# Reversing mirrored filter bins on TensorE: one 192-column matmul in place of three of 64 columns

## Chip, cores, metric

One core of a Trainium2 chip (trn2). The metric is device time in microseconds of one execution. Where I call a kernel faster or slower, the 95% interval of its ratio leaves out 1.

## The reference

The reference alternates two layers twice, each with a residual and a layer norm. Layer A is a global filter in the frequency domain, layer B a two-matmul MLP with Mish.

```python
def _A_ref(x, w_r, w_i):                     # x: 1 x 2048 x 1024
    X = rfft2(x.astype(float32), axes=(-2, -1))
    W = w_r + 1j * w_i                       # 2048 x 513, shared by both A layers
    return irfft2(X * W, s=(2048, 1024)).astype(bfloat16)
# x = x + A(layernorm(x)); x = x + B(layernorm(x)); the same once more
```

## The kernel before

The transforms are matmuls with tables. Work in the frequency domain goes in eight groups `g`, and each group needs its piece of the filter W in a certain order of bins. Of the eight bin classes of a part and a row set, VectorE copies five as they lie. The other three are mirrored: rows and bins come in reverse. The rows (partitions) are reversed by a matmul with an anti-diagonal table `jt`; it writes PSUM, and ScalarE copies that into the second half of each of the first three 128-wide runs of the filter tile `both`. This is done in the first A layer only; the second reloads the finished filter from a scratch tensor in HBM.

The filter tile `wr` is laid out per partition as `[c][s][512]`: real and imaginary part, two row sets, and 512 bins. The 512 bins are 64 blocks `i` of 8 bins `k`, so a bin's position is `8*i + k`. One block is 8 x 2 = 16 bytes. Within the kernel's SBUF buffer the tile starts at a multiple of 16 bytes.

```python
def filter_bins(self, g, ps, banks, wr, wts, off, jt, r_jt, eng):
    both = self.ARENA[:, off // 2:off // 2 + 2048]
    fns = []
    for i in range(2):                                   # row set
        src, j0 = (i, (2, 0)[i]) if g == 0 else (1 - i, 0)
        for c in range(2):                               # real, imaginary
            for kd in (1, 2, 3):                         # one bin class at a time
                col = 512 * i + 192 * c + 64 * (kd - 1)
                mov = wr.ap[:, c, src, :].rearrange("p (i k) -> p k i", k=8)[:, 7 - kd, :]
                fns.append(lambda e, col=col, j=(j0 + c) * P, mov=mov: e.matmul(
                    ps[:, col:col + 64], jt[:, j:j + P], mov, start=True, stop=True))
    self.group(fns, reads=[wr.res, r_jt], writes=banks)
    # ... VectorE copies the bins that are not mirrored (L855) ...
    for i in range(2):                                   # L859 in the profile
        src = ps[:, 512 * i:512 * i + 384].rearrange("p (c k i) -> p c k i", c=2, i=64)
        d3 = both[:, i, :, 0:384].rearrange("p c (k i) -> p c k i", i=P)
        self.op(self.act, lambda e, d3=d3, src=src: e.activation(d3[:, :, :, 64:128], src, ACT.Copy), ...)

# order of a step of the first A layer (cut)
for step in range(11):
    for h in range(2):
        s2(g2, h)                                        # L650: matmuls, then a copy out of PSUM
        if h == 0 and li == 0: filter_bins(g2)           # L844: the matmuls of this study
        s3(g3, h)                                        # L688 to L691
        i1(g4, h)                                        # L717
        i2(g5, h)                                        # L738, L756
```

`self.group` lets only the first matmul wait and only the last one signal. So in each group 12 matmuls of 64 columns run with nothing between them.

Of the kernel before, what the change touches and what calls it, by code (L numbers as in the profile page):

```python
# [5 lines left out]
ACT = mybir.ActivationFunctionType  # L6
ALU = mybir.AluOpType
P = 128
# [171 lines left out]
class KB:  # L180
# [439 lines left out]
    def layer_A(self, li):  # L620
# [177 lines left out]
        for step in range(8 + 3):  # L798
            g2, g3, g4, g5 = step, step - 1, step - 2, step - 3
            for h in range(2):  # L800
                if 0 <= g2 < 8:
                    s2(g2, h)
                if 0 <= g2 < 8 and h == 0 and li == 0:
                    filter_bins(g2)
                if 0 <= g3 < 8:
                    s3(g3, h)
                if 0 <= g4 < 8:
                    i1(g4, h)
                if 0 <= g5 < 8:
                    i2(g5, h)  # L810
                    u_turn(g5, h)
            if 0 <= g3 < 8 and g3 + 2 < 8:
                load_tabs(g3 + 2)
            if li == 0 and g2 + 2 < 8:
                load_w(g2 + 2)
            if li == 0 and 1 <= g2 < 9:
                self.keep_filter(g2 - 1)
            if li and 1 <= g2 < 5:
                load_w(g2 + 3)
            if 0 <= g4 < 8 and g4 + 2 < 8:  # L820
                load_btabs(g4 + 2)
# [12 lines left out]
# [4 lines that stand above are left out]
        for i in range(2):  # L838
            src, j0 = (i, (2, 0)[i]) if g == 0 else (1 - i, 0)
            for c in range(2):  # L840
                for kd in (1, 2, 3):
                    col = 512 * i + 192 * c + 64 * (kd - 1)
                    mov = wr.ap[:, c, src, :].rearrange("p (i k) -> p k i", k=8)[:, 7 - kd, :]
                    fns.append(lambda e, col=col, j=(j0 + c) * P, mov=mov: e.matmul(  # L844
                        ps[:, col:col + 64], jt[:, j:j + P], mov, start=True, stop=True))
        self.group(fns, reads=[wr.res, r_jt], writes=banks)
        for w in wts:
            w.res.begin()
        parts = [w.res for w in wts]
        both = both.rearrange("p (s c k) -> p s c k", s=2, c=2)  # L850
        own = wr.ap.rearrange("p c s (i k) -> p s c k i", k=8)
        for k, n, col in ((0, 4, 0), (7, 1, 448)):
            dst = both[:, :, :, col:512].rearrange("p s c (k i) -> p s c k i", k=n)[:, :, :, :, 0:64]
            src = own[:, :, :, k:k + n, :]
            self.op(eng, lambda e, dst=dst, src=src: e.tensor_copy(dst, src), reads=[wr.res], parts=parts)  # L855
        for i in range(2):
            src = ps[:, 512 * i:512 * i + 384].rearrange("p (c k i) -> p c k i", c=2, i=64)
            d3 = both[:, i, :, 0:384].rearrange("p c (k i) -> p c k i", i=P)
            self.op(self.act, lambda e, d3=d3, src=src: e.activation(d3[:, :, :, 64:128], src, ACT.Copy),  # L859
                    reads=banks, parts=parts)  # L860

    def keep_filter(self, g):
# [234 lines left out]
```

## Time and profile before

| | |
|---|---|
| time, median of 3 runs | 1071.35 us (1070.46 to 1071.45) |
| span of the profiled run | 1068.5 us |
| TensorE busy over the span | 91% |
| first A layer, 50 to 112 us: TensorE, ScalarE, VectorE busy | 100%, 89%, 75% |
| filter matmuls (L844) | 8 groups of 12 x 64 columns |
| stream time of the 8 groups, start to start | 11.0 us |

How to read it: the duration of a matmul in these traces includes a modelled end and overlaps the next one. What a group costs is the time from its first start to the first start of the next line, where TensorE never waits. I call this stream time. The lines are shown in the prediction.

### The profile page before, as it was taken

The page shows a single profiled execution, that of the slowest core. Times are in us where ns is not written, and L with a number is a line of the kernel's source. Part 1 is how long each engine was busy: PE and PEld are TensorE (multiplying, and loading weights), DVE is VectorE, ACT ScalarE, POOL GpSimd, SP SyncE. Part 2 cuts the span into 40 slices and gives each one's busy share as a digit, 9 for nine tenths or more (in the row PEclk, how much of TensorE's full clock was granted, in tenths as well). Part 3 has the DMA queues.
Part 4 walks back from the last instruction along what each step waited for, and adds up shares of the span by engine and source line. Part 5 has one row for each costly group of instructions (what it writes and reads, how often), then busy time and mean ns, then how long its engine had stood idle before and what let it go on. Part 6 is the DMA issues. An engine that isn't in the chain of part 4 may idle for free. (4 is left out here: it accounts for less than half of the span.)

```text
span 1068.5 us, 14145 instructions
## 1 busy us (share of the span) xinstructions
PE 973.0 (91%) x6089; PEld 509.6 (48%) x6089; DVE 362.4 (34%) x811; ACT 330.2 (31%) x466; POOL 55.3 (5%) x86
## 2 busy tenths in 40 slices
PE   0799479999999999999969965999999999999998
PEld 0677345444444444444427744444444444444443
DVE  7887482600444200033436866451011110000111
ACT  6898253342000234300007843434300013431000
POOL 2042000000000000001310200000000000000000
PEclk9699769999999999999988985999999999999999
DMA  9678732444000122211720885144500002210000
GB/s 293 148 247 252 186 111 85 153 150 126 20 20 21 57 68 73 79 60 38 142 47 30 229 200 139 55 143 146 169 22 20 21 34 70 74 40 11 20 20 29
DMA packets 138958, 102.80 MB, mean 96 GB/s; under 512 B 59952, under 2 KB 117552, under 8 KB 138896
## 3 DMA queue, kind: packets, MB, share of 16 engines
q1 hardware_dynamic: 128528, 78.34, 25.1%
q0 software_dynamic: 7856, 22.94, 7.6%
q10 hardware_dynamic: 2512, 0.62, 0.3%
q8 instruction: 48, 0.79, 0.3%
q14 instruction: 14, 0.11, 0.0%
HBM read 80.85 MB, written 20.71 MB: 95 GB/s over the span
## 5 line engine op out<-in xcount | busy, mean ns | idle before, releaser
L930 PE MATMUL PS<-ARENA 128*128 128x512 bf16 x1792 | 393.7, 382 | 1.6 <-DVE ARENA L917 1.6
L948 PE MATMUL PS<-ARENA 128*128 128x512 bf16 x1792 | 390.0, 379 | 0.0
L934 ACT ACTIVATE ARENA<-PS,B 128x512 bf16<-128x512 f32 x224 | 153.8, 687 | 440.0 <-PE PS L930 440.0
L930 PEld LDWEIGHTS PS<-ARENA 128*128 128x128 bf16 x1792 | 175.5, 98 | 214.3 <-issue 6.0
L948 PEld LDWEIGHTS PS<-ARENA 128*128 128x128 bf16 x1792 | 174.5, 98 | 207.8
L953 DVE TENSOR_TENSOR XS<-PS,XS 128x512 bf16<-128x512 f32 x64 | 44.3, 691 | 566.1 <-PE PS L948 566.1
L436 DVE BATCH_NORM_STATS2 BN<-XS 128x6 f32<-128x512 bf16 x108 | 69.5, 673 | 7.5 <-DMA XS<-in_A_x_dram 6.3
L875 PE MATMUL PS<-MT,ARENA 128*128 128x32 bf16 (+1 forms) x768 | 24.7, 189 | 36.1 <-DMA ARENA<-u_scratch 27.9
L881 DVE TENSOR_TENSOR XS<-PS,XS 128x512 bf16<-128x512 f32 (+1 forms) x40 | 29.1, 789 | 75.8 <-PE PS L875 75.8
L575 ACT ACTIVATE ARENA<-PS 128x1024 bf16<-128x1024 f32 x16 | 16.1, 1018 | 110.8 <-PE PS L569 110.6
L875 PEld LDWEIGHTS PS<-MT,ARENA 128*128 128x128 bf16 x768 | 23.0, 101 | 39.5 <-issue 31.4
L417 ACT ACTIVATE ARENA<-XS 128x1024 bf16<-128x1024 bf16 x20 | 21.1, 1056 | 54.6 <-DVE XS L881 43.6
L695 ACT ACTIVATE ARENA<-PS 128x1024 bf16<-128x1024 f32 x32 | 33.0, 1032 | 9.0 <-PE PS L691 9.0
L650 PE MATMUL PS<-FD,ARENA 128*128 128x256 bf16 (+1 forms) x312 | 33.5, 257 | 2.4 <-DVE ARENA L577 2.4
L724 ACT ACTIVATE ARENA<-PS 128x1024 bf16<-128x1024 f32 x32 | 33.0, 1032 | 3.7 <-PE PS L717 3.7
L717 PE MATMUL PS<-ARENA 128*128 128x256 bf16 x256 | 33.2, 273 | 0.1
L699 DVE TENSOR_TENSOR ARENA<-ARENA 128x1024 bf16<-128x1024 bf16 x32 | 22.1, 690 | 28.1 <-ACT ARENA L695 22.7
L650 PEld LDWEIGHTS PS<-FD,ARENA 128*128 128x128 bf16 x312 | 26.3, 99 | 7.2 <-DVE ARENA L577 2.8
L717 PEld LDWEIGHTS PS<-ARENA 128*128 128x128 bf16 x256 | 24.6, 98 | 9.7 <-DVE ARENA L706 0.9
L912 PE MATMUL PS<-IDENT,ARENA 128*128 128x128 bf16 x256 | 21.6, 242 | 8.3 <-DVE ARENA L479 5.8
L738 PE MATMUL PS<-ARENA,BD 128*128 128x256 bf16 x192 | 25.9, 273 | 0.4 <-DVE ARENA L764 0.2
L912 PEld LDWEIGHTS PS<-IDENT,ARENA 128*128 128x128 bf16 x256 | 18.6, 109 | 14.0 <-DVE ARENA L479 6.9
(66 smaller groups left out, 517.8 us busy)
## 6 DMA issues: line engine op xcount, KB each, us to landing
ARENA<-in_B_w_dram SPq DMA_DIRECT2D x56, 512.0 KB, 4.0
ARENA<-in_B_w_dram SPq DMA_DIRECT2D x56, 256.0 KB, 4.4
u_scratch<-ARENA SPq DMA_DIRECT2D x14, 512.0 KB, 4.1
ARENA<-u_scratch SPq DMA_DIRECT2D x14, 512.0 KB, 5.3
XS<-in_A_x_dram SPq DMA_DIRECT2D x4, 1024.0 KB, 8.6
ARENA<-in_A_x_dram SPq DMA_DIRECT2D x32, 128.0 KB, 3.3
w_scratch<-ARENA POOLq DMA_DIRECT2D x8, 512.0 KB, 5.0
ARENA<-w_scratch POOLq DMA_DIRECT2D x8, 512.0 KB, 3.6
```

Source lines behind the costliest of these rows:

```text
L436: self.op(self.dve, lambda e: e.bn_stats(self.BN[:, j, 6 * h:6 * h + 6], self.XS[:, j, 512 * h:512 * h + 512]), reads=[self.r_xs[j]], part ...
L650: fns.append(lambda e: e.matmul(dst, at(r), FD[:, t:t + dst.shape[-1] * 2], start=start, stop=stop))
L695: self.op(act, lambda e: e.activation(x.ap.rearrange("p a b -> p (a b)"), ps, ACT.Copy, scale=SIG), reads=banks, writes=[x.res])
L717: fns.append(lambda e, c=c, part=part: e.matmul(ps[:, c * 256:(c + 1) * 256], yk.ap[:, part, c * P:(c + 1) * P], t[:, (128, 0)[part]:(384, ...
L724: self.op(act, lambda e: e.activation(v.ap[:, :, i, :], src, ACT.Copy), reads=banks, parts=[v.res])
L875: fns.append(lambda e, l=l: e.matmul(ps[:, w * l:w * l + w], self.UT.ap[:, u0 + l, :], self.MT[:, 8 * lo:8 * lo + w], start=True, stop=True))
L881: self.op(self.dve, lambda e: e.tensor_tensor(xs, src, xs, ALU.add), reads=rb, parts=self.r_xs[lo:lo + nb])
L912: fns.append(lambda e, db=db: e.transpose(PSb[:, bank, db * P:(db + 1) * P], xn.ap[:, db * P:(db + 1) * P], self.IDENT[:]))
L930: fns.append(lambda e, db=db, bank=bank, fl=fl: e.matmul(PS[:, bank, :], wb.ap[:, db, fl * P:(fl + 1) * P], x.ap[:, db, :], start=(db == 0 ...
L934: self.op(act, lambda e, bank=bank, ft=ft: e.activation(at.ap[:, ft, :], PS[:, bank, :], ACT.Mish, bias=self.B1[:, ft:ft + 1]), reads=[sel ...
L948: fns.append(lambda e, i=i, ft=ft: e.matmul(PS[:, bank, :], at.ap[:, ft, t * P:(t + 1) * P], W2[ft].ap[:, h * 512:(h + 1) * 512], start=(i ...
L953: self.op(dve, lambda e: e.tensor_tensor(xs, PS[:, bank, :], xs, ALU.add), reads=[self.r_bank[bank]], writes=[self.r_xs[j]])
```

## The change

The intent is to issue fewer and wider matmuls: 32 in place of 96, and as many fewer weight loads. The three bin classes of a part and a row set share the same table, so they can be one matmul with a moving operand of 3 x 64 columns. They are adjacent bins (4, 5, 6), read in ascending order, so the copy out of PSUM writes the classes backwards.

```diff
-                for kd in (1, 2, 3):
-                    col = 512 * i + 192 * c + 64 * (kd - 1)
-                    mov = wr.ap[:, c, src, :].rearrange("p (i k) -> p k i", k=8)[:, 7 - kd, :]
-                    fns.append(lambda e, col=col, j=(j0 + c) * P, mov=mov: e.matmul(
-                        ps[:, col:col + 64], jt[:, j:j + P], mov, start=True, stop=True))
+
+                col = 512 * i + 192 * c
+                mov = wr.ap[:, c, src, :].rearrange("p (i k) -> p k i", k=8)[:, 4:7, :]
+                fns.append(lambda e, col=col, j=(j0 + c) * P, mov=mov: e.matmul(
+                    ps[:, col:col + 192].rearrange("p (k i) -> p k i", i=64), jt[:, j:j + P], mov, start=True, stop=True))
@@
-            self.op(self.act, lambda e, d3=d3, src=src: e.activation(d3[:, :, :, 64:128], src, ACT.Copy),
+            self.op(self.act, lambda e, d3=d3, src=src: e.activation(d3[:, :, ::-1, 64:128], src, ACT.Copy),
```

## The prediction

> **What bounds the kernel now.** I read four views of the profile, in this order. First the page: which engine is full, and when. The busy totals and the slices (each digit is a tenth of the busy share of 26.7 us) give the frame:
>
> ```profile
> PE 973.0 (91%) x6089; PEld 509.6 (48%) x6089; DVE 362.4 (34%) x811; ACT 330.2 (31%) x466; POOL 55.3 (5%) x86
> ...
> PE   0799479999999999999969965999999999999998
> ...
> PEclk9699769999999999999988985999999999999999
> ```
>
> TensorE is the engine to watch, but a share of the whole says nothing of one stage. The changed matmuls run only in the first spectral layer, in slices 2 to 4.
>
> Second, the groups by line, shapes kept apart. The columns are line, engine, operation, operands, shape and count, then busy us and mean ns of one:
>
> ```profile
> L844 PE MATMUL PS<-ARENA 128*128 128x64 bf16 x96 | 12.4, 294 | 0.0
> L875 PE MATMUL PS<-MT,ARENA 128*128 128x64 bf16 x256 | 10.2, 193 | 2.6 <-DVE XS L881 2.6
> L717 PE MATMUL PS<-ARENA 128*128 128x256 bf16 x256 | 33.2, 273 | 0.1
> ```
>
> The first row is the code that changes: 96 matmuls, 8 groups of 12. The second has the same shape, 128x64 with 128x128 weights, yet one takes 193 ns against 294. Even the 256-column matmul of the third is shorter (273). Something other than the count makes L844 dear.
>
> Third, the timeline of TensorE around a group of L844, with the start, the duration and the number of instructions. The modelled durations overlap, so I use starts only:
>
> ```profile
> 71.24 1.05 PE L650 MATMUL PS<-FD,ARENA 128*128 128x256 bf16 x8
> 72.12 1.55 PE L844 MATMUL PS<-ARENA 128*128 128x64 bf16 x12
> 73.50 0.40 PE L688 MATMUL PS<-ARENA 128*128 128x512 bf16 x1
> ...
> 49.17 1.58 PE L844 MATMUL PS<-ARENA 128*128 128x64 bf16 x12
> 50.57 0.39 PE L650 MATMUL PS<-FD,ARENA 128*128 128x256 bf16 x1
> ```
>
> A group takes the stream from 72.12 to 73.50, 1.38 us or 115 ns for each matmul. The very first (49.17 to 50.57) takes 1.40 us, 117 ns each.
>
> Fourth, the table of windows: the length, then busy time and count of PE, PEld, DVE, ACT and POOL, the granted clock and the DMA share:
>
> ```profile
> 50.00:112.00 62.00, 62.00 (x584) 49.38 (x583) 46.25 (x80) 54.98 (x67) 19.77 (x33) 0.99 0.76 234
> ...
> 52.26:53.64 1.38, 1.38 (x15) 1.37 (x13) 0.00 (x0) 1.27 (x2) 1.08 (x2) 1.00 0.49 125
> ...
> 89.31:90.68 1.37, 1.37 (x14) 1.37 (x12) 1.37 (x3) 1.22 (x2) 0.00 (x0) 1.00 1.02 397
> ...
> 49.17:50.57 1.40, 1.40 (x13) 1.40 (x12) 0.83 (x2) 1.02 (x1) 0.21 (x1) 0.50 0.00 0
> ```
>
> From 50 to 112 us TensorE is busy 62.00 of 62.00 us, and the waits of that engine in this window are none. So here a nanosecond of TensorE's stream is a nanosecond of the kernel, unless ScalarE (54.98, 89%) takes over. The groups take the same time with VectorE idle or full and DMA at 0.49 or 1.02, so contention does not make them slow. And the group at a granted clock of 0.50 takes the same as those at 1.00.
>
> **What the Trainium skill says.** (1) "TensorE: Matmul & The Clock Gate", section "Back-to-back issue gap", has N/2.4 + 2.5 ns as the gap of warm matmuls: 29 ns for 64 columns, 109 for 256. The trace agrees for operands that are read in sequence: eight L875 matmuls of 64 columns take 0.25 us in the chain of waits (683.02 to 683.27), 31 ns each; L650's group above takes 0.88 us for 8, 110 ns each. L844 at 115 ns does not fit. (2) The same page, section "LDWEIGHTS", gives 128/1.2 = 107 ns for a weight load, close to what L844's own loads show (117 ns), so one could take L844 for bound by its loads. But L875's loads also last about 100 ns in the trace and are pipelined at 31 ns, so a load does not cost 115 ns of the stream. (3) "SBUF — State Buffer", section "Door 1: The DMA port swizzle", note on cachelines: SBUF has 16-byte lines, successive accesses to one line run at full bandwidth, and "each access that crosses to a new line pays a penalty". The moving operand of L844 takes every eighth bf16, a step of 16 bytes: each column is a new line. No page gives the size of the penalty for a matmul; the trace gives it as (115 - 31)/64 = 1.31 ns per column, if it goes by columns.
>
> That it is a matter of reading and not of the array is what the half-clock group says: before it, at the same clock, the 256-column L650 group that starts at 47.49 takes 1.68 us for 8, 210 ns each instead of 110, while L844 keeps 117 against 115.
>
> **The change part by part.** *Removed:* in each of 8 groups, 12 matmuls and 12 loads become 4 and 4, 64 of each in all. *Added:* each matmul now has 192 columns. The diff writes the operand as (k, i), and i, with the step of 16 bytes, is still the inner one. So the stream still goes to a new line at each column: 64 lines at one k, then 64 at the next. Columns in all: 12 x 64 = 768 before, 4 x 192 = 768 after. *Moved:* the order of the three k turns round, which the ScalarE copy undoes by writing its 64-wide runs backwards. It has the same 384 elements in runs of the same length, so I expect its 488 ns to stay. The order of instructions on the other four engines is the same.
>
> Cost of a 192-column matmul: in sequence it would be 31 + (110 - 31) x 128/192 = 84 ns. With the penalty per column it is 84 + 192 x 1.31 = 335 ns, and four make 1.34 us. Against 12 x 115 = 1.38 us a group saves 0.04 us, and eight save 0.3 us. If all of the 115 ns goes by columns (1.79 ns each), 192 take 344 ns and the saving is nil. If the 31 ns are a part that each matmul pays anew beside its columns, one costs 31 + 192 x 1.31 = 282 ns, four 1.13 us, and eight groups save 8 x 0.25 = 2.0 us. I choose the first: **0.3 us saved**, all on the path because TensorE is full there. The 64 loads that go, 64 x 117 ns = 7.5 us of PEld, lie under matmuls and save nothing.
>
> **The rivals.** *A: the dear part is fixed for each matmul* (a start of a strided read, or the weight load after all). Then a 192-column matmul costs 84 + 84 = 168 ns, a group 0.67 us, and 8 x (1.38 - 0.67) = 5.7 us go; if nothing but the in-sequence pace is left, 8 x (1.38 - 4 x 0.084) = 8.4 us. For it: 115 is near the 117 of a load, and both stay put with the clock. Against it: L875 with as many loads at 31 ns. Time: 1063 to 1066 us. *B: ScalarE takes the saving.* If A holds, ScalarE's 89% allows some 7 us of TensorE's 62 to go before it is the bound, so A would mostly reach the end; for my own 0.3 us it does not matter. *C: the new form is slower*: a copy with a negative step, or a jump back of the operand between planes. The copy may grow without hurting (its consumer is a scratch store and a multiply one step later), and three jumps per matmul replace three instruction starts. At worst 0.1 us per group, about 1 us. *The ceiling:* the eight groups, read start to start, take 1.40 + 4 x 1.37 + 3 x 1.38 = 11.0 us. If they were free, the kernel would gain 11.0/1071 = 1.03%. So faster by over 2% is out of reach.
>
> **Range and chances.** The centre is 1071.35 - 0.3 = 1071.0 us. The three runs of before spread over 1.0 us, which sets the upper end: 1072.3. Downwards I give room for the case with 2.0 us: 1068.8. I give A about one chance in eight, which lies below the range; a run in a disturbed state takes the rest. Within 2%: 0.99; the sides share what is left.
>
> **What would show it right or wrong.** In the changed profile L844 should have 32 matmuls of mean duration near 294 + 128 x 1.31 = 460 to 294 + 128 x 1.79 = 523 ns (rival A: about 350 or less). From the start of a group to the start of the next line should be 1.3 to 1.4 us (A: 0.33 to 0.7), and the half-clock first group the same. L859's copies should stay near 488 ns. The distance from the first group's start to that of the last, 48.7 us now (49.17 to 97.90), should shrink by 0.3 us; 5 us would prove A. PEld busy should fall by about 7 us without any effect. I am wrong if the reader of the moving operand fetches ahead across lines within one longer matmul, so that the penalty is paid at its start only.

## The result, and the profile after

| | before | after |
|---|---|---|
| median | 1070.90 us (4 runs, 1069.44 to 1071.45) | 1070.94 us (4 runs, 1070.60 to 1071.66) |
| ratio after/before | | 1.0003, 95% interval 0.9986 to 1.0021: same |

The result is correct.

The groups by line, in the columns that the prediction explains: first the copy L859 of the kernel before, then three lines of the changed kernel:

```profile
L859 ACT ACTIVATE ARENA<-PS 128x384 bf16<-128x384 f32 x16 | 7.0, 488 | 2.4 <-PE PS L844 2.2
...
L844 PE MATMUL PS<-ARENA 128*128 128x192 bf16 x32 | 12.2, 515 | 0.0
...
L859 ACT ACTIVATE ARENA<-PS 128x384 bf16<-128x384 f32 x16 | 7.0, 488 | 2.1 <-PE PS L844 2.0
...
L844 PEld LDWEIGHTS PS<-ARENA 128*128 128x128 bf16 x32 | 3.6, 112 | 3.8 <-issue 3.5
```

A third of the matmuls is left, and their busy time is what it was: 12.2 us after 12.4. One takes 515 ns, inside the 460 to 523 that the prediction gave to a cost by columns. The reversed copy costs 488 ns, to the nanosecond what it did.

TensorE's timeline around the same group as before (start, duration), and around the first group, which runs at half clock:

```profile
71.27 1.05 PE L650 MATMUL PS<-FD,ARENA 128*128 128x256 bf16 x8
72.16 1.52 PE L844 MATMUL PS<-ARENA 128*128 128x192 bf16 x4
73.50 0.40 PE L688 MATMUL PS<-ARENA 128*128 128x512 bf16 x1
...
49.21 1.54 PE L844 MATMUL PS<-ARENA 128*128 128x192 bf16 x4
50.58 0.39 PE L650 MATMUL PS<-FD,ARENA 128*128 128x256 bf16 x1
```

A group takes 73.50 - 72.16 = 1.34 us, after 1.38. Its four matmuls take 335 ns each. The half-clock group takes 1.37 us, after 1.40.

The windows (length, then busy time and count of PE, PEld, DVE, ACT and POOL, granted clock, DMA share and GB/s):

```profile
50.00:112.00 62.00, 61.58 (x517) 42.69 (x524) 46.34 (x81) 55.08 (x67) 19.66 (x33) 0.99 0.76 234
```

The loads (PEld) lost 49.38 - 42.69 = 6.7 us of busy time here, and nothing came of it. PE shows 61.58 and not 62.00, but this is no gap: the trace reports no wait of TensorE in this window, and of the whole execution 5931 matmuls are recorded against 6025 weight loads, so some records are missing.

### The profile page after: what moved, and what is told of

Its sections match the earlier page's. It is cut to its first block, busy times and chain, and to the rows that moved or that the text cites. A ratio compares the mean times of both kernels' runs of the same rounds, so it can differ in the third digit from the quotient of the medians.

```text
span 1068.8 us, 13923 instructions
## 1 busy us (share of the span) xinstructions
PE 965.8 (90%) x5931; PEld 501.8 (47%) x6025; DVE 362.8 (34%) x811; ACT 330.2 (31%) x466; POOL 55.2 (5%) x86
## 5 line engine op out<-in xcount | busy, mean ns | idle before, releaser
L650 PE MATMUL PS<-FD,ARENA 128*128 128x256 bf16 (+1 forms) x312 | 33.6, 257 | 2.4 <-DVE ARENA L577 2.4
L650 PEld LDWEIGHTS PS<-FD,ARENA 128*128 128x128 bf16 x312 | 26.4, 100 | 7.7 <-DVE ARENA L577 2.8
L479 DVE TENSOR_SCALAR ARENA<-XS,RS 128x1024 bf16<-128x1024 bf16 x48 | 24.9, 550 | 0.8
```

Of the source, the lines that this page charges most:

```text
L650: fns.append(lambda e: e.matmul(dst, at(r), FD[:, t:t + dst.shape[-1] * 2], start=start, stop=stop))
```

## The experiments

After the result two readings of the 1.75 ns that a column costs (335/192) were left, and one rival. **Theory L:** the moving operand pays for each new 16-byte line of SBUF, whatever the columns in it. **Rival C:** it pays for each column of a pattern that is not read in sequence. **Rival A** of the prediction (a fixed cost of each matmul or weight load) looked dead, but it had not been tested apart. All of these kernels start from the changed one. Every stream time below is from first start to next line's start of a group that does not wait, at full clock.

### order_actread: the same columns, neighbours inside

```diff
-mov = wr.ap[:, c, src, :].rearrange("p (i k) -> p k i", k=8)[:, 4:7, :]
-... ps[:, col:col + 192].rearrange("p (k i) -> p k i", i=64)
+mov = wr.ap[:, c, src, :].rearrange("p (i k) -> p i k", k=8)[:, :, 4:7]
+... ps[:, col:col + 192].rearrange("p (i k) -> p i k", i=64)
 # the copy L859
-src = ps[:, ...].rearrange("p (c k i) -> p c k i", c=2, i=64)
+src = ps[:, ...].rearrange("p (c i k) -> p c k i", c=2, i=64)
```

> Correct result. The 192-column operand is read with the three neighbouring bins (k) as the inner dimension and the step of 16 bytes outside, so three columns come from each 16-byte line; the ScalarE copy (L859) puts the order right by reading PSUM with a step of three floats. Theory L (a penalty for each new 16-byte line): 64 lines instead of 192, so 84 + 64 x 1.31 = 168 ns for each matmul, a group of four 0.67 us instead of 1.34, and 8 x 0.67 = 5.4 us of TensorE's stream saved: some 1065.5 us. Rival C (every column of a pattern with more than one step costs 1.7 ns, whatever line it is in): 335 ns, 1.34 us a group, no change, 1071 us. L859 was 488 ns; if strided PSUM reads cost ScalarE, it shows here alone.

Measured: correct, 1063.98 us median of 5 (before 1071.14 of 9), ratio 0.9938 (0.9925 to 0.9950). TensorE's timeline of this kernel:

```profile
69.62 0.61 PE L844 MATMUL PS<-ARENA 128*128 128x192 bf16 x4
70.07 0.38 PE L688 MATMUL PS<-ARENA 128*128 128x512 bf16 x1
```

and the windows of its first group, at half clock, and of the one just shown:

```profile
49.17:49.84 0.67, 0.67 (x6) 0.53 (x5) 0.67 (x2) 0.43 (x1) 0.48 (x1) 0.50 0.00 0
69.62:70.07 0.45, 0.45 (x6) 0.38 (x4) 0.41 (x2) 0.45 (x2) 0.00 (x0) 1.00 0.97 382
```

The same 192 columns, the same table, the same number of instructions: 0.45 us a group in place of 1.34. Rival C is out. Theory L holds, but my figure for it was too high: 0.45/4 = 113 ns a matmul, not 168. I had added the cost of the lines (64 x 1.31) to that of the columns (84). What fits is 64 lines at 1.76 ns and nothing beside them: the columns add nothing as long as the lines are the slower of the two. At half clock the order turns. The window of the first group of step1 (the next run), whose columns are read in sequence:

```profile
49.15:49.79 0.64, 0.64 (x6) 0.60 (x5) 0.64 (x2) 0.40 (x1) 0.58 (x1) 0.50 0.00 0
```

In sequence 192 columns take 0.64/4 = 160 ns at half clock, here 0.67/4 = 168: the lines, 113 ns, hide. (The estimate is 192/1.2 = 160 ns; 1.2 GHz is half of the 2.4 GHz that the Trainium skill gives in "TensorE: Matmul & The Clock Gate", section "What's actually happening", and the trace shows 0.50 beside both groups.) The line rate doesn't follow the array's clock: the changed kernel's group takes 1.37 us at 0.50 and 1.34 at 1.00. The column rate does: step1's takes 0.64 and 0.33.

For the end, the last of the eight groups, in the kernel before and in this one:

```profile
97.90 1.55 PE L844 MATMUL PS<-ARENA 128*128 128x64 bf16 x12
99.27 0.40 PE L688 MATMUL PS<-ARENA 128*128 128x512 bf16 x1
...
92.57 0.62 PE L844 MATMUL PS<-ARENA 128*128 128x192 bf16 x4
93.03 0.38 PE L688 MATMUL PS<-ARENA 128*128 128x512 bf16 x1
```

L688 starts 6.2 us earlier (99.27 - 93.03), and the whole span is 6.3 us shorter (1068.5 and 1062.2).

### step1: read in sequence

```diff
-mov = wr.ap[:, c, src, :].rearrange("p (i k) -> p k i", k=8)[:, 4:7, :]
+mov = wr.ap.rearrange("p c s d -> p (c s d)")[:, 0:192].rearrange("p (k i) -> p k i", i=64)
```

> Wrong result on purpose (other columns are read). The changed kernel, but the 192 columns are read in sequence, step 2 bytes. Both L and C: 84 ns for each matmul, 0.34 us a group instead of 1.34, 8.0 us of TensorE's stream saved. If the dear part were not the reading of the moving operand but the matmul's write or its weight load, the group would stay at 1.34 us. For the end: if TensorE is the bound here, some 1063 us; if ScalarE (89% busy) takes over, less is saved than 8 us, 1064 to 1067 us.

Measured: a wrong result, 1064.05 us median of 5, ratio 0.9938 (0.9925 to 0.9950).

```profile
69.59 0.49 PE L844 MATMUL PS<-ARENA 128*128 128x192 bf16 x4
69.92 0.38 PE L688 MATMUL PS<-ARENA 128*128 128x512 bf16 x1
```

0.33 us a group, 83 ns a matmul, against 84 expected. So all that is dear in the changed kernel is the way in which its moving operand is read. The time shows no gain from the last 0.12 us a group: 1064.05 against 1063.98 with order_actread, well inside both intervals. In the traces the last group ends 0.5 us sooner (92.51 against 93.03) and the span is 0.3 us shorter (1061.9, 1062.2), which is less than the noise. It is not 8 x 0.12 = 1.0 us, in part because the second and the fourth group take 0.45 and 0.61 us here too: the matmul after them starts late. Some waits of step1's weight loads from 50 to 112 us (who waited for whom, us in total, times, the longest):

```profile
PEld PS L717 <- DVE ARENA L706: 0.8, 2, 0.4
PEld PS L717 <- DVE ARENA L699: 0.7, 2, 0.4
...
PEld PS L688 <- ACT ARENA L695: 0.3, 1, 0.3
```

In the kernel before, neither a matmul nor a weight load waited for another engine in this stage. Once TensorE's stream is shorter, its loads begin to wait, in step1 2.5 us for VectorE and 0.5 for ScalarE. In order_actread they already wait 2.6 us in all, so these waits set both kernels apart from the one before, and not from each other. How the rest divides between waits and noise these runs do not settle.

### seq64x12: twelve narrow matmuls, read in sequence

```diff
-mov = wr.ap[:, c, src, :].rearrange("p (i k) -> p k i", k=8)[:, 4:7, :]
-fns.append(... one matmul, 192 columns)
+for k in range(3):
+    mov = wr.ap[:, c, src, 64 * k:64 * k + 64]
+    fns.append(... one matmul, 64 columns, ps[:, col + 64 * k:col + 64 * k + 64])
```

> Wrong result on purpose. Twelve matmuls of 64 columns in each group, as in the kernel before, but each read in sequence. My reading: 31 ns each as with L875, 0.37 us a group instead of 1.38, little more than the 0.33 us of four wide ones, so that the number of matmuls and weight loads is worth 0.04 us a group. Rival A (a fixed cost of each matmul or its weight load, some 115 ns): stays at 1.38 us.

Measured (one look; the result is wrong as intended; the edit moves the matmul to line 845):

```profile
70.30 0.51 PE L845 MATMUL PS<-ARENA 128*128 128x64 bf16 x12
70.64 0.38 PE L688 MATMUL PS<-ARENA 128*128 128x512 bf16 x1
```

Twelve matmuls and twelve loads take 0.34 us, 28 ns each, where those of the kernel before took 115; the other groups that do not wait take 0.34 to 0.36 us, up to 30 ns each. Against step1's 0.33 us, the fusion of three into one is worth 0.01 to 0.03 us a group. Rival A is out: neither the number of matmuls nor their loads were the cost.

### step2, step4, step16: how many columns share a line

```diff
-mov = wr.ap[:, c, src, :].rearrange("p (i k) -> p k i", k=8)[:, 4:7, :]
+flat = wr.ap.rearrange("p c s d -> p (c s d)")
+step2:  mov = flat[:, 0:384].rearrange("p (k i t) -> p k i t", i=64, t=2)[:, :, :, 1]
+step4:  mov = flat[:, 0:256].rearrange("p (i k) -> p k i", k=4)[:, 0:3, :]
+step16: mov = flat[:, 0:1024].rearrange("p (i k) -> p k i", k=16)[:, 0:3, :]
```

> Wrong result on purpose. 192 columns in one matmul as in the changed kernel, step of 4 bytes, so four columns in each 16-byte line, 48 lines. The runs so far: in sequence 0.33 us a group (83 ns a matmul, 24 lines), three columns to a line 0.45 us (113 ns, 64 lines), one to a line 1.34 us (335 ns, 192 lines); 113/64 and 335/192 are both about 1.75 ns a line. Line theory (the slower of 0.41 ns a column and 1.75 ns a line): 48 lines hide under the columns, 83 to 85 ns, 0.33 us a group. Rival D (any step other than one element costs): well above that, towards 0.45 us or more.

> Wrong result on purpose. Step of 8 bytes, two columns in each 16-byte line, 96 lines. Line theory at 1.75 ns a line: 168 ns a matmul, 0.67 us a group. The Trainium skill's note that two hits in a line are enough for full bandwidth would have 83 ns, 0.33 us. Rival D (cost by column for any step): 1.34 us.

> Wrong result on purpose. Step of 32 bytes, every second line is skipped; 192 columns, 192 lines. Line theory: as in the changed kernel, 335 ns a matmul, 1.34 us a group. Rival E (the cost grows with the distance in bytes, as if the bytes between were read too): about twice, 2.7 us a group.

(The note that the second of these texts names, and the page that order_pewrite's names below, are "SBUF — State Buffer", section "Door 1: The DMA port swizzle", note on cachelines. It says that at least two hits on a line are needed; that two are enough is a reading of it.)

Measured, one look each, all with a wrong result as intended. TensorE's timeline of step2 (4 bytes):

```profile
68.77 0.51 PE L844 MATMUL PS<-ARENA 128*128 128x192 bf16 x4
69.12 0.38 PE L688 MATMUL PS<-ARENA 128*128 128x512 bf16 x1
```

of step4 (8 bytes):

```profile
69.94 0.85 PE L844 MATMUL PS<-ARENA 128*128 128x192 bf16 x4
70.61 0.40 PE L688 MATMUL PS<-ARENA 128*128 128x512 bf16 x1
```

and of step16 (32 bytes):

```profile
73.40 1.54 PE L844 MATMUL PS<-ARENA 128*128 128x192 bf16 x4
74.76 0.40 PE L688 MATMUL PS<-ARENA 128*128 128x512 bf16 x1
```

All readings of a 192-column matmul together; a line visit is a change of line in the order of reading:

| kernel | columns per line visit | line visits | stream time of a group | one matmul | per line visit |
|---|---|---|---|---|---|
| step1 | 8 | 24 | 0.33 us | 83 ns | (hidden) |
| step2 | 4 | 48 | 0.35 us | 87 ns | (1.8 ns) |
| order_actread | 3 | 64 | 0.45 us | 113 ns | 1.76 ns |
| step4 | 2 | 96 | 0.67 us | 168 ns | 1.74 ns |
| after | 1 | 192 | 1.34 us | 335 ns | 1.74 ns |
| step16 | 1, each second line | 192 | 1.36 us | 340 ns | 1.77 ns |

The theory fits within 5%: at full clock a matmul's stream time is the larger of 0.43 ns a column (83/192) and 1.75 ns a line visit. Rival D is out (step2 is not dear), and so is rival E (twice the distance costs 1.5% more, not twice). The table also fits no other length of a line, if lines are what counts: with 8 bytes, step4 would cost as much as the changed kernel (168 ns against 335); with 32 bytes, step16 would cost double (340 against 335). Of the numbers tried, four columns per line visit are the fewest at nearly full speed (87 ns against 83).

### order_actwrite and order_pewrite: who puts the order right

With the columns in the order (i, k), someone must turn them back. In order_actread ScalarE reads PSUM with a step of three floats. Two other forms:

```diff
 # order_actwrite: ScalarE reads in sequence and scatters its writes
+src = ps[:, ...].rearrange("p (c i k) -> p c i k", c=2, i=64)
+d3 = both[:, i, :, 0:384].rearrange("p c (k i) -> p c i k", i=P)
+... e.activation(d3[:, :, 64:128, ::-1], src, ACT.Copy)
 # order_pewrite: TensorE writes PSUM with a step of 64 floats, the copy stays as in the changed kernel
+... ps[:, col:col + 192].rearrange("p (k i) -> p i k", i=64)
```

> Correct result. TensorE as in the run order_actread: theory L 0.67 us a group and some 5.4 us saved, rival C no change. Here the ScalarE copy reads PSUM in sequence and scatters its writes (bf16, one element in each run of 64). If strided writes cost ScalarE, L859 goes well above 488 ns here and not there; ScalarE is busy for 55 of 62 us in this stage, so 16 copies that are 0.5 us longer would take most of the saving.

> Correct result. TensorE reads in the order of order_actread but writes PSUM with a step of 64 floats, so that the ScalarE copy is that of the changed kernel, word for word (488 ns). If strided PSUM writes slow matmuls (the Trainium skill, SBUF page, says so of any non-contiguous PSUM access), the group takes more than the 0.67 us of theory L, perhaps as much as 1.34 us; if not, this is the cheapest form, some 1065.5 us.

order_actwrite: correct, 1084.24 us median of 4, ratio 1.0120 (1.0104 to 1.0135), so slower than the kernel before. Its groups by line, and the window of the stage:

```profile
L859 ACT ACTIVATE ARENA<-PS 128x384 bf16<-128x384 f32 x16 | 29.3, 2124 | 0.0
```

```profile
50.00:112.00 62.00, 48.73 (x400) 32.90 (x399) 35.61 (x63) 61.11 (x56) 19.05 (x32) 0.94 0.61 192
```

TensorE has the short groups here too, but the copy takes 2124 ns for the same 384 elements a partition, 1.6 us more where I had allowed for 0.5. The durations of these copies overlap, so ScalarE's added busy time is 29.3 - 7.0 = 22 us. It is full now (61.11 of 62), while TensorE falls to 48.73. The bound has moved. The copy's innermost dimension is also only three elements long; whether that or the scatter of the writes is dear, this run does not separate.

order_pewrite: correct, 1064.88 us median of 5, ratio 0.9944 (0.9932 to 0.9957).

```profile
69.11 0.81 PE L844 MATMUL PS<-ARENA 128*128 128x192 bf16 x4
69.74 0.40 PE L688 MATMUL PS<-ARENA 128*128 128x512 bf16 x1
```

0.63 us a group, 157 ns a matmul against 113: the strided PSUM writes cost 44 ns a matmul, less than I allowed for. In order_actread the copy L859 has a mean of 551 ns where it had 488 (first line; the second is step1's):

```profile
L859 ACT ACTIVATE ARENA<-PS 128x384 bf16<-128x384 f32 x16 | 7.4, 551 | 0.0
...
L859 ACT ACTIVATE ARENA<-PS 128x384 bf16<-128x384 f32 x16 | 7.5, 555 | 0.0
```

That is no cost of its strided PSUM reads: step1 has the very copy of the changed kernel and shows 555. In both kernels no copy waits for TensorE any longer, and they queue behind one another. I did not test that explanation apart.

## Why the prediction was right

- **The bound in the stage** was read rightly. In order_actread the eight groups take 0.67 + 0.47 + 0.45 + 0.61 + 4 x 0.45 = 4.0 us of the stream (the fourth with a wait in it), after 11.0: 7.0 us less. In the profiled executions the stage ends 6.2 us sooner and the span is 6.3 us shorter, so some 0.8 us is lost to waits within the stage and the rest of what TensorE saves here reaches the end. The time fell by 1071.14 - 1063.98 = 7.2 us by the medians, 0.62% of 1071 = 6.6 us by the ratio (5.4 to 8.0 by its interval).
- **What makes L844 dear** was read rightly from the kernel before: the twin of the same shape at 31 ns, the indifference to the clock and the step of 16 bytes. The experiments confirm each: 28 ns in seq64x12, the line rate at both clocks, and the step in the table. The indifference to the clock alone would not have told reading from a fixed cost; step1 and seq64x12 do.
- **The cost after** was 335 ns predicted, 335 measured; a group 1.34 us predicted, 1.34 measured. Summed over the eight groups the stream shortened by about 0.26 us (11.02 to 10.76, one group's end inferred because the record of the matmul after it is missing), against 0.3 predicted. In the time this can't be seen: the interval of the ratio is 0.35% wide, 3.8 us. A saving anywhere from nil to 2.0 us would have landed in the predicted range, so that the time fell there speaks only against rival A; the rest is settled by the trace.
- **One mark was missed**: the distance from the first group to the last was to shrink by 0.3 us and shrank by 0.11 (48.73 to 48.62). From the second group on it did shrink, by 0.20 (45.64 to 45.44). Between the first two lie 16 matmuls of L650 in the transition from half to full clock, which took 1.81 us after 1.69.
- **The form of the cost was not quite right.** The prediction took 0.41 ns a column plus 1.31 ns for each new line. The two terms do not add, the larger one counts. With one column per line both forms give 1.72 to 1.75 ns, so the prediction could not fail by it. It failed where lines and columns part: I expected 168 ns of order_actread and got 113. The lower and the upper case of the prediction (0 and 2.0 us saved) came from the same doubt; the intercept of a straight line through 115 ns at 64 and 335 ns at 192 columns is 5 ns, so there is little fixed cost.
- **Rivals.** A fell to the result and to seq64x12. B did not matter for the change. Where TensorE's stream was cut further (order_actread, step1), waits did appear, but mostly for VectorE, which the prediction did not name; ScalarE became the bound only in order_actwrite, whose copy is four times as long. C did not come: the copy stayed at 488 ns.

## What to carry to other kernels

Before you fuse matmuls, compare their stream time with that of a matmul of the same shape elsewhere in the trace; if they are slower, count the 16-byte lines that the moving operand visits, not the instructions. Put at least four neighbouring bf16 in the innermost dimension where the layout allows, or as many as there are (three gave 113 ns instead of 335), and let the reader of PSUM restore the order. Do not let ScalarE's copy scatter single bf16 writes for it in the form of order_actwrite: the copy grew fourfold and took the bound. Here order_actread is correct and beats the kernel before by about 0.6%, and so the changed kernel too, which takes the same time.

## What the Trainium skill lacked or had wrong

- "SBUF — State Buffer", section "Door 1: The DMA port swizzle", note on cachelines: it says that at least two hits on a 16-byte line are needed for full bandwidth, and not how many suffice; two do not. For the moving operand of a bf16 matmul of 192 columns at full clock two columns per line take 168 ns against 83 in sequence, three 113, four 87. So a step of 4 bytes is nearly free, and one of 8 bytes is not.
- The same note gives no size for the penalty. These runs show 1.74 to 1.77 ns for each line visit, the same at a granted clock of 0.50 and 1.00 (1.37 and 1.34 us for four matmuls of 192 visits), in place of the time of the columns and not on top of it.
- "TensorE: Matmul & The Clock Gate", section "Back-to-back issue gap": the page gives N/2.4 + 2.5 ns for a lone matmul and says that among weight loads it under-counts at small N (81 ns measured at 128 columns). In these traces each matmul has a weight load of its own, and the formula holds for operands read in sequence: 83 ns at 192 columns, 28 to 31 at 64. The page doesn't say that it needs that order; with a step of 16 bytes the gaps are 335 and 115.
- "PSUM — Partial Sum Buffer", table row "Cachelines": any access pattern with gaps slows matmuls. This agrees, and the size here is 157 ns against 113 with 192 floats written at a step of 64. The row says nothing of engines that read: ScalarE's copy with a step of three floats took 551 ns, and one in sequence under the same queueing 555.
- I found no page with the cost of scattered ScalarE writes: 2124 ns against 488 to 555 for a copy of 384 elements a partition, when neighbouring writes are single bf16 in different runs (and the innermost dimension is three long, which no run separates from the scatter).
